# Attention and ELU MLP on one core: a later table for blocks 0 and 1, other weight portions, and the first batch's work spread otherwise over the engines

## The chip, the core and the metric

The kernel runs on one core of a Trainium2 chip. The metric is device time in microseconds (us), the median of several executions. A separate execution was recorded by the profiler; its views (busy time, waits, the chain of waits, the timeline) are what the prediction reads. Engines are named as in the profile: PE (matmul; PEld its weight loads), DVE (VectorE), ACT (ScalarE), POOL (GpSimd) and SP, which here only issues DMAs.

## What is computed

```
q, k, v: [8, 8, 576, 64] f32 (batch, heads, sequence, head dim)
q_s = softmax(q) over the 64 of head dim
k_s = softmax(k) over the sequence
kv  = k_s^T v                      # 64 x 64 per batch and head
x   = q_s kv, heads side by side   # 4608 x 512
h   = x @ w_in                     # w_in 512 x 2048
g   = h if h > 0 else exp(h) - 1
out = g @ w_out                    # w_out 2048 x 512, f32
```

## The kernel before

**Tiling.** A batch has 576 rows of q, k and v: 512 main rows as 128 partitions of four (R = 4), and 64 rest rows. Heads 0 to 3 are part A, heads 4 to 7 part B, the rest rows part R ("M" is A and B together, "C" is B and R). The MLP runs in nine blocks j: blocks 0 to 7 take the 512 main rows of a batch, block 8 the rest rows of all batches (XTR). A block has 16 steps s, one for each 128 columns of the hidden layer.

**A step.** `hidden` (L520): four matmuls into a bank of HB (three banks), exp on ACT into ES (L528), ES - 1 on POOL (L529). `elu` (L544): DVE combines bank and ES into GT (L550). `project` (L554): four matmuls into the four banks OB, three steps later (LAG = 3). A bank of HB comes free with the GT of its chunk, so `hidden` of step s waits for `elu` of step s - 3. At a block's end `store` copies the four banks on ACT and DVE and sends them.

**The next batch, beside these steps.** While block j runs, batch j + 1 is prepared. For k: `kmax` on DVE (per part A or B three instructions of 128x256, L198 to L203; for R two of 64x256, L209) into KA; `kturn` on PE (L218) into the shared bank AB; `kacross` (DVE, L226) takes the maxima over the turned partitions into NM; `kdiag` (DVE, L241) writes them on diagonals, DG; `kspread` (PE, L249) spreads them back; `ksub` (DVE, L261, L268), `kexp` (ACT, L278). `vconv` (ACT, L344, L348) casts v to VB. `kv_mm` (PE, L367) makes kv in the bank AB, `kv_fac` (DVE, L380, L384) scales and masks it into MB. For q: `qmax` (DVE, L403), `qsub` (POOL, L411), `qexp` (ACT, L417), `qsum` (DVE, L421, L423), `qmul` and `qmul_rest` (POOL, L434, L440) into QS and QSR; `qturn` (SP, L450, L454) is a DMA transpose into QW and QWR, `qwide` (ACT, L485, L489) widens that into QT and QTR; `attend` (PE L495, copy L501) makes a fourth of XT, `attend_rest` (L509, L514) the part of XTR.

**Order.** Every engine runs its instructions in the order in which the program emits them; waits are on semaphores that a small table of readers and writers puts in. The order is written out by hand: `first_batch` (L762) for batch 0, and then per step `hidden`, `project`, `step_pe`, `early`, `store`, `attend_rest`, `elu`, the weights, and one of `step_late` (blocks 0 and 1) and `step` (later blocks), `step_ahead` (block 1 on). In the first batch k is subtracted on PE (`kraw_first`, `kmin_first`) and q turned on PE (`qturn_first`, `qwide_first`).

**Queues.** SP issues the loads of q, k and v, the transposes and the stores, in order. POOL issues the weights (`load_w1`, `load_w2`; the arguments are the first and last chunk), between its own instructions. KR and QR have two buffers, VR has one.

Of the kernel before, what the change touches and what calls it, by code (L numbers as in the profile page):

```python
# [3 lines left out]
AF = mybir.ActivationFunctionType  # L4
# [5 lines left out]
F16 = mybir.dt.float16  # L10

B, H, S, D = 8, 8, 576, 64
# [3 lines left out]
R = 4  # L16
# [7 lines left out]
AB = 7  # L24
# [11 lines left out]
class Gen:  # L36
# [297 lines left out]
    def vconv(self, b, part, en="act"):  # L334
        a = self.E["act"]
        VR = self.VR[0]
        if part in "AB":
            h0 = 0 if part == "A" else 4
            vv = VR[:, 4 * h0:4 * h0 + 16, :].rearrange("p (h r) d -> p h r d", r=R)
            out = self.VB[:, :, h0:h0 + 4, 0:64].rearrange("p r h d -> p h r d")  # L340
            if en == "gp":
                self.op("gp", lambda: self.E["gp"].tensor_copy(out, vv), [f"VR0{part}"], [f"VB{part}"])  # L342
                return
            self.op("act", lambda: a.activation(out, vv, AF.Copy), [f"VR0{part}"], [f"VB{part}"])  # L344
        else:
            for i in range(2):
                sl = slice(64 * i, 64 * i + 64)
                self.op("act", lambda: a.activation(self.VBR[sl, i, :, 0:64],  # L348
                                                    VR[sl, 32:36, :], AF.Copy),
                        [f"VR0R{i}"], [f"VBR{i}"])  # L350
# [106 lines left out]
    def qturn_first(self, part, bank):  # L457

        pe = self.E["pe"]
        hh = 0 if part == "A" else 1  # L460
        ps = self.bank[bank][:, :].bitcast(F16)

        def mm():
            for j in range(2):
                for r in range(R):
                    o = (j * R + r) * 128
                    last = pe.transpose(ps[:, o:o + 128], self.QS[hh][:, r, 2 * j:2 * j + 2, :]
                                        .rearrange("p u d -> p (u d)"), self.ID16[:, :])
            return last
        self.op("pe", mm, [f"QS{part}", "ID16"], [f"bank{bank}"])  # L470

    def qwide_first(self, part, bank):
        a = self.E["act"]
        hh = 0 if part == "A" else 1
        src = self.bank[bank][:, :].bitcast(F16).rearrange("p (j t) -> p j t", j=2)
        self.op("act", lambda: a.activation(self.QT[:, 2 * hh:2 * hh + 2, :], src, AF.Copy),
                [f"bank{bank}"], [f"QT{part}"])

    def qwide(self, part):
        a = self.E["act"]  # L480
# [105 lines left out]
    def early(self, j, s):  # L586

        if j + 1 < B:
            if s == (1 if j < 2 else 0):
                self.kacross()  # L590
            if s == (2 if j < 2 else 1):
                self.kdiag()
            if s == 9:
                self.kv_fac("A", AB)
            if s == 10:
                self.kv_fac("B", AB)

    def step_pe(self, j, s):
        n = j + 1
        if j == 0 and s == 8:  # L600
            self.attend_rest(0, AB)
        if n < B:
            if s == (1 if j < 2 else 0):
                self.kturn()
            if s == (3 if j < 2 else 4):
                self.kspread()
            if s == 9:
                self.kv_mm("A", AB)
            if s == 10:
                self.kv_mm("B", AB)  # L610
            if s >= 12:
                self.attend(n, s - 12, AB)

    def weights_last(self, s):
        if s == 0:
            self.load_w1(10, 13)
        if s == 1:
            self.load_w1(13, 16)
        if s == 2:
            self.load_w2(10, 16)  # L620

    def step_late(self, j, s):

        n, m = j + 1, j + 2
        if s == 0:
            if j == 1:
                self.kmax(n, "B")
            self.kmax(n, "R")
            if j == 0:
                self.qmax(0, "R")  # L630
        if s == 1:
            if j == 1:
                self.qwide("R")
            self.qmax(n, "A")
            if j == 0:
                self.qsub(0, "R")
        if s == 2:
            if j == 0:
                self.qexp(0, "R")
            self.qmax(n, "C")  # L640
            self.qsub(n, "A")
        if s == 3:
            self.vconv(n, "A")
            if j == 0:
                self.qsum(0, "R")
            else:
                self.load("K", 3, "MR")
            self.ksub(n, "A")
            self.qsub(n, "C")
        if s == 4:  # L650
            self.qexp(n, "A")
            self.ksub(n, "B")
            if j == 0:
                self.qmul_rest(0)
            else:
                self.load("Q", 3, "MR")
        if s == 5:
            self.kexp(n, "A")
            self.vconv(n, "R")
            self.ksub(n, "R")  # L660
            if j == 0:
                self.qturn("R")
        if s == 6:
            self.qexp(n, "C")
            self.qsum(n, "A")
        if s == 7:
            self.kexp(n, "B")
            if j == 0:
                self.qwide("R")
            self.qsum(n, "C")  # L670
            self.qmul(n, "A")
        if s == 8:
            self.kexp(n, "R")
            self.vconv(n, "B")
        if s == 9:
            self.qturn("A")
            if j == 1:
                self.load("V", m, "MR")
            self.qmul(n, "B")
        if s == 10:  # L680
            self.qmul_rest(n)
        if s == 11:
            self.qwide("A")
            self.qturn("B")
            self.qturn("R")
        if s == 13:
            self.qwide("B")
        if j == 0:
            if s == 11:
                self.load("K", 2, "MR")  # L690
            if s == 12:
                self.load("Q", 2, "MR")
            if s == 13:
                self.load("V", 2, "RM")
            if s == 15:
                self.kmax(2, "A")

    def step(self, j, s):
        n, m = j + 1, j + 2
# [62 lines left out]
    def first_batch(self):  # L762

        self.kraw_first("A", (0, 1))
        self.kmax(0, "A")
        self.kmax(0, "B")
        self.kmax(0, "R")
        self.qmax(0, "A")
        self.qsub(0, "A")
        self.kturn()  # L770
        self.kraw_first("B", (2, 3))
        self.kraw_first("R", (4,))
        self.kacross()
        self.kdiag()
        self.kmin_first("A", (0, 1))
        self.kmin_first("R", (4,))
        self.kmin_first("B", (2, 3))
        self.vconv(0, "R")
        self.qexp(0, "A")
        self.qmax(0, "B")  # L780
        self.load_w1(0, 3)
        self.qsub(0, "B")
        self.kexp_first("A", (0, 1))
        self.kexp_first("R", (4,))
        self.qsum(0, "A")
        self.qmul(0, "A", "dve")
        self.vconv(0, "A", "gp")
        self.load_w2(0, 2)
        self.vconv(0, "B", "gp")
        self.load_w1(3, 6)  # L790
        self.load("V", 1, "RM")
        self.qexp(0, "B")
        self.kexp_first("B", (2, 3))
        self.qturn_first("A", 5)
        self.qwide_first("A", 5)
        self.qsum(0, "B")
        self.qmul(0, "B")
        self.kv_mm("A", 7)
        self.kv_fac("A", 7)
        self.kv_mm("B", 4)  # L800
        self.attend(0, 0, 5)
        self.attend(0, 1, 7, "dve")
        self.kv_fac("B", 4)
        self.load_w2(2, 6)
        self.load_w1(6, 10)
        self.qturn_first("B", 6)
        self.qwide_first("B", 6)
        self.attend(0, 2, 3)
        self.attend(0, 3, 4, "dve")
        for c in range(len(HB)):  # L810
            self.hidden_mm(0, c, range(2))
        self.load_w2(6, 10)

    def program(self):
        self.alloc()
# [5 lines left out]
        self.load("Q", 1, "MR")  # L821
        self.init()
        self.first_batch()
        self.kmax(1, "A")
        self.kmax(1, "B")

        steps = [(j, s) for j in range(B + 1) for s in range(NCH)]
        for i in range(len(steps) + LAG):
# [5 lines left out]
                self.project(pj, ps)  # L834
            if i < len(steps):
                self.step_pe(j, s)
                self.early(j, s)
            if i >= LAG and ps == NCH - 1:
                self.store(pj)
            if i < len(steps):  # L840
                if 0 < j < B and s == 2:
                    self.attend_rest(j, AB)
                self.elu(j, s)
                if j == 0 and s < 3:
                    self.weights_last(s)
                if j < 2:
                    self.step_late(j, s)
                else:
                    self.step(j, s)
                if j > 0:  # L850
                    self.step_ahead(j, s)
# [38 lines left out]
```

## Time and profile before

| | us |
|---|---|
| device time, median of 3 runs | 338.16 (336.59 to 339.66) |
| device time of the profiled execution | 338.62 |
| its span, first to last instruction | 336.8 |
| PE busy | 310.1 (92%) |
| DVE, ACT, POOL busy | 233.3, 188.0, 170.2 |
| first exp of block 0 (ACT L528) | 28.60 |
| first GT of block 0 (DVE L550) | 30.02 |
| first matmuls of block 1, of block 2 | 66.65, 104.56 |

The busy shares are means over the whole span. The prediction reads them by stage, since only the first two blocks are edited.

### The profile page before, as it was taken

To read this page: it belongs to the slowest core of one execution; us is meant where nothing else is said; L and a number is where in the kernel's file an instruction comes from. 1 tells how busy PE (TensorE), PEld (TensorE's weight loads), DVE (VectorE), ACT (ScalarE), POOL (GpSimd) and SP (SyncE) were. 2 spreads that over 40 slices of the span, in tenths; PEclk is the share of its full clock that TensorE was granted. 3 is DMA by queue.
4 is the path that set the end of the run, shared out by engine and by line. 5 is a ranking of instruction groups with operands and counts; after the bars stand their busy time and mean duration, and the time that the engine had idled before them with its cause. 6 is when DMAs were issued, how large, how long until landed. Compare 5 with 4: busy or idle time off the path is not lost.

```text
span 336.8 us, 4143 instructions
## 1 busy us (share of the span) xinstructions
PE 310.1 (92%) x1447; PEld 245.1 (73%) x1447; DVE 233.3 (69%) x382; ACT 188.0 (56%) x298; POOL 170.2 (51%) x204
## 2 busy tenths in 40 slices
PE   4677869979998999999999999999999999999993
PEld 1355647767776888787878887888788778888882
DVE  5937784388988797978897789778977344335342
ACT  1542484637647855686568557856785553334331
POOL 1784855227662666366537653755465333333330
PEclk9957998999999999999999999999999999999998
DMA  8999983958798367436733682371033011003003
GB/s 247 315 339 355 379 213 70 287 137 247 190 207 254 125 170 190 133 127 171 208 113 126 172 235 86 125 184 28 9 116 63 10 65 63 0 0 127 0 0 126
DMA packets 65173, 50.60 MB, mean 150 GB/s; under 512 B 31360, under 2 KB 57984, under 8 KB 65152
## 3 DMA queue, kind: packets, MB, share of 16 engines
q1 hardware_dynamic: 60080, 41.43, 44.4%
q0 software_dynamic: 4752, 8.39, 8.3%
q10 hardware_dynamic: 320, 0.52, 0.5%
q8 instruction: 11, 0.18, 0.2%
q14 instruction: 10, 0.08, 0.1%
HBM read 36.70 MB, written 9.44 MB: 137 GB/s over the span
## 4 chain that ended last, share of the span: by engine, by line
PE 77%; DMA 12%; DVE 6%; ACT 2%; POOL 1%; issue 1%; SPq 1%; DVEq 0%
PE bank L540 35%; PE bank L560 35%; DMA VR<-in_v_dram 6%; DMA QW<-QS 2%; PE bank L367 2%; PE bank L495 2%; DMA QWR<-QSR 2%; DMA KR<-in_k_dram 2%; DVE QM L403 1%; PE bank L218 1%; PE bank L509 1%; DVE GT L550 1%; DVE DG L241 1%; DVE QZ L421 1%; POOL QS L434 1%
## 5 line engine op out<-in xcount | busy, mean ns | idle before, releaser
L529 POOL TENSOR_SCALAR ES<-ES 128x512 f32<-128x512 f32 x144 | 92.5, 643 | 144.8 <-ACT ES L528 144.7
L560 PE MATMUL bank<-W2S,GT 128*128 128x512 f32 x576 | 155.6, 392 | 0.4 <-DVE OSB L571 0.4
L550 DVE SCALAR_TENSOR_TENSOR GT<-bank,ES 128x512 fp32r<-128x512 f32 x144 | 98.4, 683 | 73.0 <-PE bank L540 53.3
L540 PE MATMUL bank<-XT,W1S 128*128 128x512 f32 x512 | 144.4, 403 | 1.0 <-DVE GT L550 1.0
L528 ACT ACTIVATE ES<-bank 128x512 f32<-128x512 f32 x144 | 86.1, 598 | 104.9 <-PE bank L540 104.2
L560 PEld LDWEIGHTS bank<-W2S,GT 128*128 128x128 f32 x576 | 108.6, 189 | 24.4 <-DVE OSB L571 1.1
L540 PEld LDWEIGHTS bank<-XT,W1S 128*128 128x128 f32 x512 | 95.4, 191 | 23.0 <-ACT XT L501 3.0
L411 POOL TENSOR_TENSOR QR<-QR,QM 128x1024 f32<-128x1024 f32 (+2 forms) x17 | 34.7, 2042 | 11.0 <-DVE QM L403 10.9
L434 POOL TENSOR_TENSOR QS<-QR,QI 128x1024 f16<-128x1024 f32 x15 | 28.6, 1907 | 2.1 <-DVE QI L423 2.0
L501 ACT ACTIVATE XT<-bank 128x512 fp32r<-128x512 f32 x30 | 18.0, 599 | 15.8 <-PE bank L495 15.1
L403 DVE TENSOR_REDUCE QM<-QR 128x16 f32<-128x1024 f32 (+2 forms) x17 | 21.6, 1273 | 0.1
L421 DVE TENSOR_REDUCE QZ<-QR 128x16 f32<-128x1024 f32 (+2 forms) x17 | 21.6, 1272 | 0.0
L417 ACT ACTIVATE QR<-QR 128x1024 f32<-128x1024 f32 (+2 forms) x17 | 18.8, 1104 | 1.6 <-POOL QR L411 1.5
L344 ACT ACTIVATE VB<-VR 128x1024 bf16<-128x1024 f32 x14 | 14.8, 1059 | 5.1 <-DMA VR<-in_v_dram 5.0
L540 PE MATMUL bank<-XTR,W1S 128*128 128x512 f32 x64 | 17.1, 389 | 0.0
L261 DVE TENSOR_TENSOR KR<-KR,bank 128x1024 f32<-128x1024 f32 x14 | 16.9, 1208 | 0.0
L495 PE MATMUL bank<-QT,MB 128*128 128x512 f32 x32 | 14.0, 449 | 2.7 <-ACT QT L485 1.4
L198 DVE TENSOR_TENSOR KA<-KR 128x256 f32<-128x256 f32 x16 | 14.6, 911 | 2.5 <-DMA KR<-in_k_dram 2.5
L485 ACT ACTIVATE QT<-QW 128x1024 fp32r<-128x1024 f16 x14 | 14.7, 1051 | 1.5 <-DMA QW<-QS 1.5
L278 ACT ACTIVATE EK<-KR 128x1024 bf16<-128x1024 f32 x14 | 14.7, 1050 | 0.0
L540 PEld LDWEIGHTS bank<-XTR,W1S 128*128 128x128 f32 x64 | 12.0, 188 | 2.5
L367 PE MATMUL bank<-VB,EK 128*128 128x132 bf16 x128 | 12.5, 239 | 0.9 <-POOL VB L342 0.6
(62 smaller groups left out, 186.5 us busy)
## 6 DMA issues: line engine op xcount, KB each, us to landing
out_dram<-OSB SPq DMA_DIRECT2D x32, 256.0 KB, 2.8
KR<-in_k_dram SPq DMA_DIRECT2D x7, 1024.0 KB, 5.9
QR<-in_q_dram SPq DMA_DIRECT2D x7, 1024.0 KB, 7.8
VR<-in_v_dram SPq DMA_DIRECT2D x7, 1024.0 KB, 6.2
W1S<-in_moe_w_in_dram POOLq DMA_DIRECT2D x4, 768.0 KB, 10.8
W2S<-in_moe_w_out_dram POOLq DMA_DIRECT2D x2, 1024.0 KB, 12.7
W2S<-in_moe_w_out_dram POOLq DMA_DIRECT2D x1, 1536.0 KB, 14.7
KR<-in_k_dram SPq DMA_DIRECT2D x2, 512.0 KB, 4.5
```

The costliest lines, as they stand in the source:

```text
L367: pe.matmul(o, self.EK[:, r, h:h + 2, :].rearrange("p u d -> p (u d)"), self.VB[:, r, h:h + 2, :].rearrange("p u c -> p (u c)"), start=(r ...
L403: self.op("dve", lambda: v.tensor_reduce(self.QM[:, g], QR[:, g, :], AX.X, ALU.max), self.qkeys(b, part), self.qstat("QM", part))
L411: self.op("gp", lambda: e.tensor_tensor(QR[:, g, :], QR[:, g, :], m, ALU.subtract), keys + self.qstat("QM", part), keys)
L417: self.op("act", lambda: a.activation(QR[:, g, :], QR[:, g, :], AF.Exp), keys, keys)
L421: self.op("dve", lambda: v.tensor_reduce(self.QZ[:, g], QR[:, g, :], AX.X, ALU.add), self.qkeys(b, part), self.qstat("QZ", part))
L434: self.op(en, lambda: e.tensor_tensor(out, src, z, ALU.mult), keys[:1] + [f"QI{part}"], [f"QS{part}"])
L495: self.op("pe", lambda: pe.matmul(self.bank[bank][:, :], mb, self.QT[:, f, :], start=True, stop=True), [f"MB{f}", f"QT{part}"], [f"bank{ba ...
L528: self.op("act", lambda: a.activation(ES[:, :], ps, AF.Exp), [f"bank{bank}"], [ek])
L529: self.op("gp", lambda: g.tensor_scalar(ES[:, :], ES[:, :], -1.0, 1.0, ALU.add, ALU.mult), [ek], [ek])
L540: return pe.matmul(ps, self.W1S[:, kc, c * 128:(c + 1) * 128], x[:, kc, :], start=(kc == 0), stop=(kc == 3))
L550: self.op("dve", lambda: v.scalar_tensor_tensor(self.GT[n % NG][:, :], ps, 0.0, ES[:, :], ALU.max, ALU.min), [f"bank{bank}", ek], [f"GT{n ...
L560: return pe.matmul(self.bank[OB[t]][:, :], self.GT[n % NG][:, t * 128:(t + 1) * 128], self.W2S[:, c, :], start=(c == 0), stop=(c == NCH - 1))
```

## The change

Blocks 0 and 1 get other steps for most of the next batch's work: the k maxima stand in steps 0 (A), 1 (B) and 2 (R) instead of before the steps and in 0, or at the end of the block before; `kturn` in 4 (was 1), `kacross`, `kdiag` and `kspread` in 5 (were 1, 2 and 3), the `kv` pair in 10 and 11 (was 9 and 10). `kacross` and `kdiag` of step 5 are emitted ahead of `kspread` and of the step's `elu`. The casts of v, the q work and some loads move along.

In the first batch, `kdiag` goes to ACT (four instructions), the two casts of v from POOL to DVE, `qmul` of part A from DVE to POOL and of part B from POOL to DVE, the copy of `attend` 1 from DVE to ACT. The rest rows of q are prepared before the steps, not in steps 0 to 7; they are turned on PE in step 2 (not by a DMA) and attended in step 3 (was 8). The six early `hidden_mm` stand ahead of attends 2 and 3.

The weights are issued in ten loads instead of nine: three before the steps (were six), the others in steps 0, 1, 3, 6 and 7.

```diff
--- before.py
+++ after.py
@@ -338,8 +338,8 @@
             h0 = 0 if part == "A" else 4
             vv = VR[:, 4 * h0:4 * h0 + 16, :].rearrange("p (h r) d -> p h r d", r=R)
             out = self.VB[:, :, h0:h0 + 4, 0:64].rearrange("p r h d -> p h r d")
-            if en == "gp":
-                self.op("gp", lambda: self.E["gp"].tensor_copy(out, vv), [f"VR0{part}"], [f"VB{part}"])
+            if en == "dve":
+                self.op("dve", lambda: self.E["dve"].tensor_copy(out, vv), [f"VR0{part}"], [f"VB{part}"])
                 return
             self.op("act", lambda: a.activation(out, vv, AF.Copy), [f"VR0{part}"], [f"VB{part}"])
         else:
@@ -457,24 +457,30 @@
     def qturn_first(self, part, bank):
 
         pe = self.E["pe"]
-        hh = 0 if part == "A" else 1
         ps = self.bank[bank][:, :].bitcast(F16)
+        src = self.QSR[:, :, :].unsqueeze(1) if part == "R" else self.QS["AB".index(part)][:, :, :, :]
+        n = src.shape[1]
 
         def mm():
             for j in range(2):
-                for r in range(R):
-                    o = (j * R + r) * 128
-                    last = pe.transpose(ps[:, o:o + 128], self.QS[hh][:, r, 2 * j:2 * j + 2, :]
+                for r in range(n):
+                    o = (j * n + r) * 128
+                    last = pe.transpose(ps[:, o:o + 128], src[:, r, 2 * j:2 * j + 2, :]
                                         .rearrange("p u d -> p (u d)"), self.ID16[:, :])
             return last
         self.op("pe", mm, [f"QS{part}", "ID16"], [f"bank{bank}"])
 
     def qwide_first(self, part, bank):
         a = self.E["act"]
-        hh = 0 if part == "A" else 1
-        src = self.bank[bank][:, :].bitcast(F16).rearrange("p (j t) -> p j t", j=2)
-        self.op("act", lambda: a.activation(self.QT[:, 2 * hh:2 * hh + 2, :], src, AF.Copy),
-                [f"bank{bank}"], [f"QT{part}"])
+        ps = self.bank[bank][:, :].bitcast(F16)
+        if part == "R":
+            out = self.QTR[:, :, :].rearrange("p (hh j) t -> p j hh t", hh=2)
+            src, key = ps[:, 0:256].rearrange("p (j hh t) -> p j hh t", j=2, hh=2), "QTR"
+        else:
+            hh = 0 if part == "A" else 1
+            out, key = self.QT[:, 2 * hh:2 * hh + 2, :], f"QT{part}"
+            src = ps[:, :].rearrange("p (j t) -> p j t", j=2)
+        self.op("act", lambda: a.activation(out, src, AF.Copy), [f"bank{bank}"], [key])
 
     def qwide(self, part):
         a = self.E["act"]
@@ -586,96 +592,93 @@
     def early(self, j, s):
 
         if j + 1 < B:
-            if s == (1 if j < 2 else 0):
+            late = j < 2
+            if s == (5 if late else 0):
                 self.kacross()
-            if s == (2 if j < 2 else 1):
+            if s == (5 if late else 1):
                 self.kdiag()
-            if s == 9:
+            if s == (10 if late else 9):
                 self.kv_fac("A", AB)
-            if s == 10:
+            if s == (11 if late else 10):
                 self.kv_fac("B", AB)
 
     def step_pe(self, j, s):
         n = j + 1
-        if j == 0 and s == 8:
+        if j == 0 and s == 2:
+            self.qturn_first("R", 6)
+            self.qwide_first("R", 6)
+        if j == 0 and s == 3:
             self.attend_rest(0, AB)
         if n < B:
-            if s == (1 if j < 2 else 0):
+            late = j < 2
+            if s == (4 if late else 0):
                 self.kturn()
-            if s == (3 if j < 2 else 4):
+            if s == (5 if late else 4):
+                if late:
+                    self.early(j, s)
                 self.kspread()
-            if s == 9:
+            if s == (10 if late else 9):
                 self.kv_mm("A", AB)
-            if s == 10:
+            if s == (11 if late else 10):
                 self.kv_mm("B", AB)
             if s >= 12:
                 self.attend(n, s - 12, AB)
 
-    def weights_last(self, s):
+    def weights(self, s):
         if s == 0:
-            self.load_w1(10, 13)
+            self.load_w2(3, 6)
         if s == 1:
-            self.load_w1(13, 16)
-        if s == 2:
-            self.load_w2(10, 16)
+            self.load_w1(6, 9)
+        if s == 3:
+            self.load_w2(6, 9)
+            self.load_w1(9, 12)
+        if s == 6:
+            self.load_w1(12, 16)
+            self.load_w2(9, 12)
+        if s == 7:
+            self.load_w2(12, 16)
 
     def step_late(self, j, s):
 
         n, m = j + 1, j + 2
         if s == 0:
-            if j == 1:
-                self.kmax(n, "B")
-            self.kmax(n, "R")
-            if j == 0:
-                self.qmax(0, "R")
+            self.kmax(n, "A")
         if s == 1:
             if j == 1:
                 self.qwide("R")
+            self.kmax(n, "B")
+        if s == 2:
+            self.kmax(n, "R")
+        if s == 3:
+            self.vconv(n, "R")
             self.qmax(n, "A")
-            if j == 0:
-                self.qsub(0, "R")
-        if s == 2:
-            if j == 0:
-                self.qexp(0, "R")
+            if j == 1:
+                self.load("K", 3, "MR")
+        if s == 4:
+            self.vconv(n, "A")
             self.qmax(n, "C")
             self.qsub(n, "A")
-        if s == 3:
-            self.vconv(n, "A")
-            if j == 0:
-                self.qsum(0, "R")
-            else:
-                self.load("K", 3, "MR")
+        if s == 5:
+            self.vconv(n, "B")
             self.ksub(n, "A")
             self.qsub(n, "C")
-        if s == 4:
+        if s == 6:
             self.qexp(n, "A")
             self.ksub(n, "B")
-            if j == 0:
-                self.qmul_rest(0)
-            else:
+        if s == 7:
+            self.qexp(n, "C")
+            self.ksub(n, "R")
+            self.qsum(n, "A")
+            if j == 1:
                 self.load("Q", 3, "MR")
-        if s == 5:
+        if s == 8:
             self.kexp(n, "A")
-            self.vconv(n, "R")
-            self.ksub(n, "R")
-            if j == 0:
-                self.qturn("R")
-        if s == 6:
-            self.qexp(n, "C")
-            self.qsum(n, "A")
-        if s == 7:
-            self.kexp(n, "B")
-            if j == 0:
-                self.qwide("R")
             self.qsum(n, "C")
             self.qmul(n, "A")
-        if s == 8:
+        if s == 9:
             self.kexp(n, "R")
-            self.vconv(n, "B")
-        if s == 9:
+            self.kexp(n, "B")
             self.qturn("A")
-            if j == 1:
-                self.load("V", m, "MR")
             self.qmul(n, "B")
         if s == 10:
             self.qmul_rest(n)
@@ -683,6 +686,8 @@
             self.qwide("A")
             self.qturn("B")
             self.qturn("R")
+            if j == 1:
+                self.load("V", m, "MR")
         if s == 13:
             self.qwide("B")
         if j == 0:
@@ -692,8 +697,6 @@
                 self.load("Q", 2, "MR")
             if s == 13:
                 self.load("V", 2, "RM")
-            if s == 15:
-                self.kmax(2, "A")
 
     def step(self, j, s):
         n, m = j + 1, j + 2
@@ -771,45 +774,47 @@
         self.kraw_first("B", (2, 3))
         self.kraw_first("R", (4,))
         self.kacross()
-        self.kdiag()
+        self.kdiag("act")
         self.kmin_first("A", (0, 1))
         self.kmin_first("R", (4,))
         self.kmin_first("B", (2, 3))
-        self.vconv(0, "R")
+        self.qmax(0, "B")
+        self.qsub(0, "B")
         self.qexp(0, "A")
-        self.qmax(0, "B")
         self.load_w1(0, 3)
-        self.qsub(0, "B")
         self.kexp_first("A", (0, 1))
         self.kexp_first("R", (4,))
+        self.vconv(0, "R")
         self.qsum(0, "A")
-        self.qmul(0, "A", "dve")
-        self.vconv(0, "A", "gp")
-        self.load_w2(0, 2)
-        self.vconv(0, "B", "gp")
-        self.load_w1(3, 6)
+        self.qmul(0, "A")
+        self.vconv(0, "A", "dve")
+        self.vconv(0, "B", "dve")
         self.load("V", 1, "RM")
         self.qexp(0, "B")
         self.kexp_first("B", (2, 3))
+        self.kv_mm("A", 7)
+        self.kv_fac("A", 7)
         self.qturn_first("A", 5)
         self.qwide_first("A", 5)
         self.qsum(0, "B")
-        self.qmul(0, "B")
-        self.kv_mm("A", 7)
-        self.kv_fac("A", 7)
+        self.qmul(0, "B", "dve")
+        self.load_w2(0, 3)
+        self.load_w1(3, 6)
         self.kv_mm("B", 4)
+        self.kv_fac("B", 4)
         self.attend(0, 0, 5)
-        self.attend(0, 1, 7, "dve")
-        self.kv_fac("B", 4)
-        self.load_w2(2, 6)
-        self.load_w1(6, 10)
+        self.attend(0, 1, 7)
         self.qturn_first("B", 6)
         self.qwide_first("B", 6)
+        self.qmax(0, "R")
+        self.qsub(0, "R")
+        for c in range(len(HB)):
+            self.hidden_mm(0, c, range(2))
         self.attend(0, 2, 3)
         self.attend(0, 3, 4, "dve")
-        for c in range(len(HB)):
-            self.hidden_mm(0, c, range(2))
-        self.load_w2(6, 10)
+        self.qexp(0, "R")
+        self.qsum(0, "R")
+        self.qmul_rest(0)
 
     def program(self):
         self.alloc()
@@ -821,8 +826,6 @@
         self.load("Q", 1, "MR")
         self.init()
         self.first_batch()
-        self.kmax(1, "A")
-        self.kmax(1, "B")
 
         steps = [(j, s) for j in range(B + 1) for s in range(NCH)]
         for i in range(len(steps) + LAG):
@@ -834,15 +837,16 @@
                 self.project(pj, ps)
             if i < len(steps):
                 self.step_pe(j, s)
-                self.early(j, s)
+                if not (j < 2 and s == 5):
+                    self.early(j, s)
             if i >= LAG and ps == NCH - 1:
                 self.store(pj)
             if i < len(steps):
                 if 0 < j < B and s == 2:
                     self.attend_rest(j, AB)
                 self.elu(j, s)
-                if j == 0 and s < 3:
-                    self.weights_last(s)
+                if j == 0:
+                    self.weights(s)
                 if j < 2:
                     self.step_late(j, s)
                 else:
```

## The prediction

> **What bounds the kernel now.** I read the table of busy time by stage first. Columns: the stretch, its length, busy time of PE, PE's weight loads, DVE, ACT and POOL, the granted clock, the DMA share and the GB/s.
>
> ```profile
> 0.00:28.40 28.40, 18.38 (x69) 11.64 (x70) 18.69 (x41) 9.81 (x14) 14.45 (x20) 0.79 1.08 305
> 28.40:62.00 33.60, 26.45 (x123) 20.15 (x122) 21.74 (x36) 17.55 (x28) 20.56 (x23) 0.93 0.87 244
> 62.00:92.00 30.00, 27.59 (x128) 21.14 (x126) 22.83 (x38) 18.76 (x31) 15.56 (x17) 1.00 0.79 215
> ...
> 124.97:157.95 32.98, 32.98 (x162) 26.57 (x162) 27.65 (x44) 22.36 (x35) 19.09 (x22) 1.00 0.54 156
> ```
>
> From 125 us PE is busy all of a block's 32.98 us. So whatever the change saves or costs in blocks 0 and 1, which it alone edits, arrives at the end unchanged. In the timeline the matmuls of block 1 step 0 (after the fourth "attend") begin at 66.65, those of block 2 at 104.56: block 1 takes 37.9, 4.9 over the later block. Second view: PE's own waits from 28 to 125 us.
>
> ```profile
> PE bank L218 <- DVE KA L209: 4.1, 2, 2.4
> PE bank L509 <- ACT QTR L489: 2.9, 1, 2.9
> PE bank L495 <- ACT QT L485: 1.4, 1, 1.4
> PE bank L540 <- DVE GT L550: 1.0, 1, 1.0
> ```
>
> The k turn waits for the k maxima once per block (2.4 at 29.4, 1.7 at 70.8); the remainder's attention waits 2.9 at 46.5; late q transposes cost 1.4 at 100.7. The 1.0 at 41.5 goes back to ACT, which stood 4.95 us before the V cast. The chain of waits says for what:
>
> ```profile
> 19.95 19.50 DMA VR<-in_v_dram
> ...
> 42.33 6.46 DMA QWR<-QSR
> ```
>
> Batch 1's V needs 19.5 us to land, since 3 MB of weights are issued from POOL at 21.6 to 23.1 and share the DMA engines. The second line is the remainder's DMA transpose, behind the 2.9 us wait. A table of 2 us stretches shows that wait's second price:
>
> ```profile
> 50.00:52.00 2.00, 2.00 (x7) 1.53 (x7) 0.69 (x1) 1.99 (x4) 0.42 (x1) 0.62 0.59 113
> 52.00:54.00 2.00, 2.00 (x14) 1.48 (x13) 0.00 (x0) 0.14 (x1) 1.78 (x2) 0.53 0.09 18
> ```
>
> After it the clock is at about half for some 3.7 us: 1.85 us lost. Last, the timeline, for two DVE instructions beside one POOL instruction each:
>
> ```profile
> 9.75 1.90 POOL L411 TENSOR_TENSOR QR<-QR,QM 128x1024 f32<-128x1024 f32 x1 [7.80 <-DVE QM L403]
> 10.35 1.85 DVE L241 TENSOR_TENSOR DG<-ID,NM 128x512 fp32r<-128x512 f32 x1
> ...
> 97.15 1.91 POOL L411 TENSOR_TENSOR QR<-QR,QM 128x1024 f32<-128x1024 f32 x1 [0.19 <-DVE QM L403]
> ...
> 97.67 1.67 DVE L198 TENSOR_TENSOR KA<-KR 128x256 f32<-128x256 f32 x1
> ```
>
> L241 alone takes 0.68, L198 0.42; both here end just after POOL's instruction.
>
> **First batch.** The 1.85 of kdiag goes from DVE to four ACT copies of 128x128. Nearest ACT rows: 0.41 (128x256), 0.60 (x512), 1.05 (x1024), so about 0.3 each, 1.2 in all (at most 4 x 0.41 = 1.64). DVE is free at 10.3, so qmax B ends at 11.6 and POOL's qsub B follows qsub A: 11.65 to 13.55. The first W1 load moves behind it, from 11.59 to 13.55; its kind landed in 8.5 to 9 us, so about 22.3. Its first user comes at about 22.4: no cost, up to 0.5 otherwise. POOL's two V casts (2.02 and 1.05) go to DVE: between 0.7 (half of L261's 1.21 and a start) and 1.21; I take 0.9. qmul A goes to POOL (1.9), qmul B to DVE (1.62 beside POOL in the trace, 1.2 alone by L261). The chain to QS B on DVE: qsum A ends 14.3, V cast 0.9, POOL's qmul A holds it 1.9, V cast 0.9, kv_fac A 0.8, qsum B 1.45, qmul B 1.4: 21.65, as now (21.66). From there the six early matmuls fill the 1.0 us widening and the first exp comes about 6.2 later instead of 6.9. The remainder's sub, exp, sum and multiply now stand before the steps: qmul_rest ends at about 28.55 and POOL's first ES after it, so the first GT starts at 29.2 instead of 30.02. Gain 0.8 (0 to 1.7).
>
> **Block 0 up to the spread.** The new order puts this on DVE before kdiag of step 5: five GTs (0.69), six k maxima of 0.42, two of 0.42 for the rest, qmax 1.21 and 1.48, kacross 0.69, kdiag 0.68: 10.9. Consecutive ones overlap (three maxima take 1.13, not 1.26), so 10.1. The maxima have both inputs in SBUF and run beside POOL's ES (0.62): I add 0.3 for each third, 0.9, bounds 0 and 4.6 (the longest L198, L200, L203, L209 rows: 1.67, 0.83, 0.71, 0.75). kdiag ends at 29.2 + 11.0 = 40.2. PE has until then three hidden and three project groups, turn and remainder, done by about 36.4; it waits 3.8 us, and chunk 6 starts at 40.65 against 39.58 now: 1.1 lost. What is queued behind kspread on PE is everything, and ksub on DVE waits for it too.
>
> **Block 0 after it.** Now: 66.65 - 39.58 = 27.1 us. Work in it: ten steps of 1.82, two kv of 0.6, four attends of 0.23: 20.3. Gone are the wait for V (its rivals on the DMA engines are now 2.25 MB, then loads issued from step 0; with some 9 MB at 350 GB/s it lands by 29, its cast comes after 32), the 2.9 us, since the remainder is turned by PE in step 2 (two transposes by L467's 0.13, one copy of 0.4) and attended in step 3. Not gone: the half clock after a 3.8 us wait, 1.85. New: QS A comes some 10 us after kspread (ksub, GT, qsum and two weight issues on POOL before it), the transpose lands 3.0 to 7.8 later (its range), the copy takes 1.05; attend needs it 14.3 after. I take 0.5 (0 to 4.6), as it is nearest to the 3.2 median. So 20.3 + 2.35 = 22.6, and block 1 starts at 63.25 instead of 66.65: 3.4 gained.
>
> **Weights.** Ten issues instead of nine, 0.75 to 0.98 each on POOL. They delay ES in steps 0, 1, 3, 6 and 7 by up to 1.6; DVE is behind by more than that, so nothing, or 0.8 if DVE catches up. W1 6 to 9 is issued at about 31 and needed at 40.6; no load of this size took above 13.1 when all ran together.
>
> **Block 1.** PE reaches the spread after six steps of 1.82, turn 0.42, remainder 0.35, the XT wait 0.28 and the store's wait 0.4: 12.3. DVE starts its first GT 2.65 after the block (matmul, exp, ES), does the same 10.1 and two store copies (1.28): 14.0, plus 0.6 for POOL. PE waits 2.3. The late transposes of 100.7 had V's load issued before them; now V comes behind them in SP's queue; 0.4 left. Excess 2.7 instead of 4.9: 2.2 gained. Moving K and Q loads on SP costs nothing: K3 is first used at step 12. With batch 2's K sent at about 55 and the K loads' median of 5.9, its maxima (66 on) don't wait.
>
> **Sum.** 3.4 + 2.2 = 5.6 from the profiled execution's 338.62 (span 336.8, 1.8 around it): 333.0. That execution is 0.46 above the median, so 332.6.
>
> [...]
>
> **The rivals.** *Only kdiag is caught.* In step 5, counted from qmax A's end, DVE reaches kdiag after GT 0.6, qmax C 1.4 and kacross 0.66: 2.66. POOL reaches qsub C after qsub A 1.9 and ES 0.62, with hops 2.65. A tie: if POOL is first, kdiag waits some 2.0 of its 2.34. For it: 10.35 above; against: at 34.88 kdiag came first and POOL waited. Once: 334.6; in both blocks, with the half clock in block 1 as well, 338.5. *The lock at every maximum* (slower): with the longest rows each block pays 3.9 for six, 0.7 for two and 1.17 for kdiag: 5.8 instead of the 1.5 I took for both. 332.6 - 1.5 + 11.6, and 1.85 of half clock in block 1: 344.5. It turns to slower by 1% from about 5 us per block. For it: L198's median in the trace is 0.82; against: in blocks 0 and 1 POOL has only ES of 0.62 in steps 0 to 2. *V or transposes stay late:* V landing at 39 again, or the transpose at 7.8, costs 4 to 5: 337.
>
> **Chances.** Forecast, with its better bounds (no half clock, no lock: down to 328.5): 0.56. Kdiag caught once 0.08, half of that under 334.8. Caught twice or late transfers 0.2. Lock everywhere 0.16. What a measurement can tell is about 1%, 3.4 us: faster 0.6, within 0.24, slower 0.16. The range 328.5 to 341.5 leaves out most of the last case and little below.
>
> **What would show it.** Right: V no longer in the chain, no wait of PE at L509 behind QTR, a wait at L249 for kdiag of 2 to 4 us in each of blocks 0 and 1, GT of chunk 0 near 29.2, block 1 starting near 63, block 2 near 99. Wrong: kdiag ending after 42, maxima above 0.8, weights in PE's waits, ACT waiting for QW by several us.

## The result, and the profile after

The changed kernel takes 340.83 us (median of 17 runs, 339.21 to 342.16) against 338.16 of the kernel before (17 runs): a ratio of 1.0069, 95% interval 1.0045 to 1.0093. By the ratio it is slower by about 2.3 us; the forecast was 332.6. The profiled execution took 340.83, its span is 339.0.

The table of busy time by stage of the changed kernel (columns as before), cut where blocks 1 and 2 begin:

```profile
0.00:28.40 28.40, 18.64 (x71) 11.24 (x72) 17.17 (x38) 12.06 (x21) 10.63 (x17) 0.82 1.07 306
28.40:66.78 38.38, 30.84 (x142) 23.71 (x141) 27.63 (x41) 20.14 (x32) 23.76 (x29) 0.91 0.87 234
66.78:106.76 39.98, 35.92 (x162) 27.95 (x161) 32.88 (x50) 22.30 (x35) 20.89 (x23) 0.91 0.71 186
106.76:139.90 33.14, 33.14 (x163) 26.72 (x162) 28.17 (x46) 22.33 (x35) 18.96 (x22) 1.00 0.75 212
```

Block 1 starts at 66.78 (before 66.65) and takes 39.98 (before 37.91); from block 2 on PE is busy without a break. So all of the loss is in block 1, and what was to be gained in block 0 is not there. PE's own waits from 20 to 130 us (total, times, longest):

```profile
PE bank L249 <- DVE DG L241: 8.8, 2, 4.8
PE bank L546 <- DMA W1S<-in_moe_w_in_dram: 1.4, 1, 1.4
PE bank L546 <- DVE GT L556: 1.1, 1, 1.1
PE bank L218 <- DVE KA L209: 1.1, 1, 1.1
...
```

The waits for the remainder (2.9 in block 0) and for the late transposes of block 1 (1.4) are gone, and so is V from the chain of waits. In their place stands one wait per block at the spread, L249, for the diagonals, L241: 4.76 and 4.01. The timeline shows what the diagonals wait for, in block 0 and again in block 1:

```profile
39.41 0.61 POOL L535 TENSOR_SCALAR ES<-ES 128x512 f32<-128x512 f32 x1
39.99 2.32 POOL L411 TENSOR_TENSOR QR<-QR,QM 128x1280 f32<-128x1280 f32 x1
40.06 2.79 DVE L241 TENSOR_TENSOR DG<-ID,NM 128x512 fp32r<-128x512 f32 x1
...
42.91 0.79 PE L249 MATMUL bank<-DG,ONES 128*128 128x512 f32 x1 [4.76 <-DVE DG L241]
...
80.66 2.33 POOL L411 TENSOR_TENSOR QR<-QR,QM 128x1280 f32<-128x1280 f32 x1
80.75 2.79 DVE L241 TENSOR_TENSOR DG<-ID,NM 128x512 fp32r<-128x512 f32 x1
...
83.59 0.79 PE L249 MATMUL bank<-DG,ONES 128*128 128x512 f32 x1 [4.01 <-DVE DG L241]
```

In block 0 of the kernel before, the diagonals came first, and POOL's subtraction (there part A) 0.3 after them:

```profile
34.88 0.68 DVE L241 TENSOR_TENSOR DG<-ID,NM 128x512 fp32r<-128x512 f32 x1
35.18 2.14 POOL L411 TENSOR_TENSOR QR<-QR,QM 128x1024 f32<-128x1024 f32 x1
```

In the changed kernel POOL's second q subtraction (part C) starts 0.07 and 0.09 us ahead of the diagonals, which then take 2.79 instead of 0.68. They end 0.54 after POOL's instruction: most of their own 0.68 is still to be done when POOL's instruction ends. "The lock" is the name for this hold-up, 2.79 for 0.68, here and in the prediction. The table of 2 us stretches shows what the wait does to the clock (the third number from the right):

```profile
40.00:42.00 2.00, 0.00 (x0) 0.00 (x0) 1.97 (x2) 0.00 (x0) 2.00 (x2) 0.65 0.12 25
42.00:44.00 2.00, 1.09 (x3) 0.90 (x4) 1.71 (x3) 0.00 (x0) 0.30 (x1) 0.50 0.00 0
44.00:46.00 2.00, 2.00 (x6) 1.58 (x5) 0.97 (x1) 0.55 (x2) 0.00 (x0) 0.50 0.00 0
46.00:48.00 2.00, 2.00 (x7) 1.54 (x6) 1.15 (x2) 0.99 (x2) 1.87 (x3) 0.64 0.00 0
...
80.00:82.00 2.00, 0.00 (x0) 0.00 (x0) 1.97 (x3) 0.25 (x1) 2.00 (x3) 0.89 1.08 311
82.00:84.00 2.00, 0.41 (x1) 0.41 (x2) 2.00 (x2) 0.00 (x0) 0.99 (x1) 0.50 1.12 285
84.00:86.00 2.00, 2.00 (x6) 1.52 (x6) 1.36 (x2) 0.00 (x0) 0.00 (x0) 0.50 1.01 287
86.00:88.00 2.00, 2.00 (x6) 1.54 (x5) 0.47 (x1) 1.54 (x2) 0.62 (x1) 0.50 0.19 43
88.00:90.00 2.00, 2.00 (x9) 1.63 (x8) 1.35 (x2) 0.91 (x2) 0.23 (x1) 0.90 0.00 0
```

The granted clock falls to 0.50 of full speed, so twice the missing clock of such rows is the time at half clock: 2 x 2 x (0.35 + 0.5 + 0.5 + 0.36) = 6.84 in each of the two blocks, of which PE works 4.5 to 4.8 and so loses some 2.3.

### The profile page after: what moved, and what is told of

Its sections match the earlier page's. It is cut to its first block, busy times and chain, and to the rows that moved or that the text cites. A ratio compares the mean times of both kernels' runs of the same rounds, so it can differ in the third digit from the quotient of the medians.

```text
span 339.0 us, 4151 instructions
## 1 busy us (share of the span) xinstructions
PE 312.0 (92%) x1449; PEld 246.2 (73%) x1449; DVE 238.6 (70%) x382; ACT 189.5 (56%) x303; POOL 167.3 (49%) x203
## 4 chain that ended last, share of the span: by engine, by line
PE 80%; DVE 8%; DMA 6%; POOL 2%; issue 1%; SPq 1%; ACT 0%; DVEq 0%
PE bank L546 38%; PE bank L566 36%; DMA W1S<-in_moe_w_in_dram 3%; PE bank L501 2%; DVE QM L403 2%; PE bank L367 2%; DVE DG L241 2%; DVE GT L556 2%; DMA QR<-in_q_dram 1%; DMA QW<-QS 1%; POOL QR L411 1%; PE bank L249 1%; PE bank L515 1%; PE bank L218 1%; POOL QS L434 1%
## 5 line engine op out<-in xcount | busy, mean ns | idle before, releaser
L546 PE MATMUL bank<-XT,W1S 128*128 128x512 f32 x512 | 146.4, 406 | 2.8 <-DMA W1S<-in_moe_w_in_dram 1.4
L546 PEld LDWEIGHTS bank<-XT,W1S 128*128 128x128 f32 x512 | 96.4, 193 | 25.9 <-ACT XT L507 4.0
L411 POOL TENSOR_TENSOR QR<-QR,QM 128x1024 f32<-128x1024 f32 (+2 forms) x17 | 34.0, 2005 | 15.5 <-DVE QM L403 15.5
L198 DVE TENSOR_TENSOR KA<-KR 128x256 f32<-128x256 f32 x16 | 15.6, 978 | 2.3 <-DMA KR<-in_k_dram 2.3
L367 PE MATMUL bank<-VB,EK 128*128 128x132 bf16 x128 | 11.6, 228 | 1.8 <-DVE VB L342 1.8
```

The costliest lines, as they stand in the source:

```text
L411: self.op("gp", lambda: e.tensor_tensor(QR[:, g, :], QR[:, g, :], m, ALU.subtract), keys + self.qstat("QM", part), keys)
L546: return pe.matmul(ps, self.W1S[:, kc, c * 128:(c + 1) * 128], x[:, kc, :], start=(kc == 0), stop=(kc == 3))
```

## The experiments

The theory after the result (A): the diagonals lose a race of under 0.1 us to POOL's subtraction in each block; that costs 2.1 us, and through the longer idle time the clock. The rivals: the late place of the spread costs by itself, and another wait takes over without the lock (B); or the new first batch and weights cost (C). Every ratio is to the kernel before, on the same chip.

**The diagonals first.** POOL's second subtraction also reads DG, so that it comes behind the diagonals; nothing else is changed.

```diff
             self.ksub(n, "A")
-            self.qsub(n, "C")
+            self.qsub(n, "C", ["DG"])
```

> The changed kernel, with one wait added: in blocks 0 and 1 POOL's second q subtraction (part C) waits for the diagonals, so that DVE's diagonal instruction comes first. Theory A (the lock at the diagonals is the cost): L241 falls from 2.79 to about 0.7 in both blocks, PE's waits at L249 from 4.8 and 4.0 to about 2.6 and 1.9, and the half clock after block 1's wait (2.3 us) goes with it: 340.8 - 4.2 - 2.3 = 334.3, or 332.1 if block 0's half clock goes too, 336.6 if both stay. Rival B (the late place itself costs, another wait takes over): not under 339.

Measured: 335.25, ratio 0.9901 (0.9863 to 0.9938). The timeline of this run in block 0:

```profile
40.60 0.69 DVE L241 TENSOR_TENSOR DG<-ID,NM 128x512 fp32r<-128x512 f32 x1
...
41.35 0.50 PE L249 MATMUL bank<-DG,ONES 128*128 128x512 f32 x1 [2.67 <-DVE DG L241]
41.38 2.33 POOL L411 TENSOR_TENSOR QR<-QR,QM 128x1280 f32<-128x1280 f32 x1 [0.82 <-DVE DG L241]
```

The diagonals take 0.69 in both blocks, PE's waits fall to 2.67 and 1.93 as A said, and the time falls by 5.6 us: the 4.2 of the lock and part of the half clock. One added wait on POOL is worth more than the whole loss of the change. B falls: no wait took over. (The ten runs spread from 332.7 to 335.8, and the profiled one, 335.49, is among the longer.) The half clock is not gone but shorter:

```profile
42.00:44.00 2.00, 2.00 (x8) 1.60 (x7) 1.10 (x1) 1.21 (x2) 2.00 (x2) 0.68 0.02 5
44.00:46.00 2.00, 2.00 (x6) 1.54 (x6) 1.60 (x2) 0.33 (x1) 1.78 (x3) 0.50 0.08 6
46.00:48.00 2.00, 2.00 (x10) 1.68 (x9) 0.69 (x2) 1.76 (x2) 1.19 (x2) 0.97 0.95 304
```

That is 2 x 2 x (0.32 + 0.5 + 0.03) = 3.4 instead of 6.84; block 1 shows 3.4 too, after a wait of only 1.93.

**The diagonals on ACT.** The other way out of the lock: POOL still starts its subtraction first, but the diagonals are made by an engine beside it.

```diff
-                self.kdiag()
+                self.kdiag("act" if late else "dve")
```

> The changed kernel with the diagonals of blocks 0 and 1 written by ACT (four copies, 1.28 in the first batch's trace) and nothing else moved. [...] Rival B: not under 339.

Measured: 335.69, ratio 0.9928 (0.9900 to 0.9955). A gives 337.8 if the diagonals come 1.5 earlier in each block (340.8 - 3.0), and 335.5 if the half clock of block 1 goes as well: the time is at the better end. That POOL would not hold up ACT was the author's estimate; the trace of block 0 bears it out.

```profile
40.13 2.32 POOL L411 TENSOR_TENSOR QR<-QR,QM 128x1280 f32<-128x1280 f32 x1
40.20 1.28 ACT L235 ACTIVATE DG<-ID,NM 128x128 fp32r<-128x128 f32 x4 [2.19 <-DVE NM L226]
...
41.62 0.77 PE L249 MATMUL bank<-DG,ONES 128*128 128x512 f32 x1 [3.33 <-ACT DG L235]
```

POOL's instruction runs as long as before beside it, and ACT's four copies take the same 1.28 as in the first batch: it is DVE and POOL that exclude each other here (DVE's diagonals took 2.79 for 0.68 behind POOL's subtraction, and the subtraction 2.14 for 1.90 where the diagonals had begun 0.3 before it, at 35.18 in the kernel before), and the subtraction's mere presence does not hold up the diagonals. One half-clock stretch is left (3.4 us in block 0), none in block 1, in its profile.

**Half the change each.** First the new first batch and weights with the old step table. The edit: the old `early`, `step_pe` and `step_late`, without the rest rows' q work, and in the first batch

```diff
         self.qsub(0, "R")
+        self.kmax(1, "A")
+        self.kmax(1, "B")
         for c in range(len(HB)):
```

> The first batch and the weight portions of the change, with the step table of the kernel before (the rest rows of q prepared early as in the change, attended in step 8; the k maxima of batch 1, parts A and B, on DVE while it waits for attend 2). Theory A (only the new table costs, the rest of the change gains): the wait for V (1.0), the wait for the remainder (2.9) and its half clock (1.85) go, and the start comes 0.6 earlier: 338.2 - 6.3 = 331.9, range 330 to 334. Rival C (first batch or weights cost): not under 338.

Measured: 335.09, ratio 0.9918 (0.9884 to 0.9952). The sign is A's, and C falls for the first batch and the weights taken together; the size is 3 us short of the 331.9. PE's waits show where:

```profile
PE bank L218 <- DVE KA L209: 4.5, 2, 2.8
PE bank L546 <- DMA W1S<-in_moe_w_in_dram: 1.9, 1, 1.9
```

The waits for V and the remainder are gone, but the first weights now come 1.9 late, and the k turn of block 0 still waits 2.8. During and after that wait the clock was half for 6.84 us (30.0 to 36.9), against 3.4 in block 0 of the kernel before.

Then the new table alone, with the old first batch and weights (the mirrored edit):

> The kernel before with only the new step table (its own first batch, weights and late rest rows). Theory A: the diagonals are caught behind POOL in both blocks or at least wait as late as in the changed kernel, and V is late as before: slower than the changed kernel's 340.8, 341 to 345. Rival C: the table costs nothing, 337 to 339.

Measured: 339.55, ratio 1.0077 (1.0038 to 1.0117). Neither range held; by the ratio it can't be told apart from the changed kernel (1.0069). The race is lost in both blocks, by 0.09 and 0.08. In block 0:

```profile
42.29 2.33 POOL L411 TENSOR_TENSOR QR<-QR,QM 128x1280 f32<-128x1280 f32 x1
42.38 2.78 DVE L241 TENSOR_TENSOR DG<-ID,NM 128x512 fp32r<-128x512 f32 x1
...
45.22 0.79 PE L249 MATMUL bank<-DG,ONES 128*128 128x512 f32 x1 [5.27 <-DVE DG L241]
```

Its ten runs fall into 338.5 to 340.4 and 342.3 to 342.8, and the profile is of an upper one; what divides them was not tried. Together the two halves give: the table costs 0.8%, the rest gains 0.8%, both cost 0.7%. So the rest's gain hardly shows on top of the table. One reason is in the waits: with the table alone PE waits only 0.2 for the remainder, where the kernel before waited 2.9, so both halves take away the same wait. The rest is open. In the profiled execution the other half of the change does bring the spread of block 0 forward, from 45.22 to 42.91; no execution of the lower group was profiled.

**The first weights early.** On the first experiment's kernel, the first W1 load is again issued before POOL's second subtraction of batch 0.

```diff
         self.qmax(0, "B")
+        self.load_w1(0, 3)
         self.qsub(0, "B")
         self.qexp(0, "A")
-        self.load_w1(0, 3)
```

> Run e1 with the first W1 load issued before POOL's second q subtraction of batch 0, as in the kernel before. If the load's place cost what the profile shows, PE's wait for W1S (1.9 in e1, 1.4 in the changed kernel) falls under 0.5 and the time by about 1.4 to 333.9; part B of q comes some 0.4 later. Rival: the attends' chain is as late as the load, and nothing changes (335.3).

Measured: 331.67, ratio 0.9825 (0.9790 to 0.9861): a gain of 3.6 over the first experiment where 1.4 was expected (the two intervals lie just apart). Two lines of PE's timeline, first of the kernel with the diagonals first, then of this one:

```profile
23.06 2.93 PE L546 MATMUL bank<-XT,W1S 128*128 128x512 f32 x6 [1.86 <-DMA W1S<-in_moe_w_in_dram]
```

```profile
21.74 1.64 PE L546 MATMUL bank<-XT,W1S 128*128 128x512 f32 x6
```

The six early matmuls start 1.3 earlier and run at full clock, in 1.64 instead of 2.93. But the wait did not go as expected: 1.75 of it moved to the second W1 load, at 28 us. Most of the difference seems to lie in the clock. The profile of the first experiment shows half clock from 22.2 to 29.1 and for 3.4 us in each of the two blocks; this one shows it from 17.2 to 20.6 and for 3.4 us in block 0 alone. These are 6.8 us less at half clock, worth up to 3.4 of the 3.8 between the two profiled executions. Whether the load's place brings that about in every run, or by luck in this one, was not tried; the last section has what stood ahead of such stretches in the nine profiles.

**The maxima early.** On top, k maxima of parts A and B of batch 1 go into the time in which DVE waits for attend 2, R into step 0, those of batch 2 a step earlier.

```diff
         self.qsub(0, "R")
+        self.kmax(1, "A")
+        self.kmax(1, "B")
         for c in range(len(HB)):
...
         if s == 0:
-            self.kmax(n, "A")
-        if s == 1:
             if j == 1:
-                self.qwide("R")
-            self.kmax(n, "B")
-        if s == 2:
+                self.kmax(n, "B")
+            else:
+                self.kmax(n, "R")
+        if s == 1 and j == 1:
+            self.qwide("R")
             self.kmax(n, "R")
...
+            if s == 15:
+                self.kmax(2, "A")
```

> Run e5 with the k maxima drawn forward: batch 1's parts A and B into the time in which DVE waits for attend 2 (21.5 to 26.7), R into step 0; batch 2's part A into step 15 of block 0, B and R into steps 0 and 1. Theory (the rest of the wait at the spread is DVE's list): L249's waits fall from 2.7 and 1.9 to about 0.4 and 0.8, both half clocks go: 333.9 - 2.3 - 1.8 - 1.1 - 1.65 = 327, to 330 if the half clocks stay. Rival (another wait takes over at the same step, such as POOL's ES or the exp): 333 or more.

Measured: 330.38, ratio 0.9797 (0.9756 to 0.9838), not clearly apart from the run before it. The waits at the spread fell only to 1.83 and 1.70, and one half-clock stretch stayed. The time in which DVE waits had been read in the changed kernel; in the kernel that was edited it is much shorter. DVE's copy of the last part of XT, first in the changed kernel, then in the run with the first weights early:

```profile
26.68 0.69 DVE L504 CAST XT<-bank 128x512 fp32r<-128x512 f32 x1 [5.23 <-PE bank L501]
```

```profile
23.89 0.69 DVE L504 CAST XT<-bank 128x512 fp32r<-128x512 f32 x1 [1.58 <-PE bank L501]
```

The maxima now stand before this copy, and PE waits 0.84 for it, so that the first GT starts at 27.94 instead of 26.60 in the run before: of the 2.3 us that the expectation took from DVE's list ahead of the spread, 1.3 are given back at its beginning. No wait took over at the spread itself; a new one came ahead of it.

**A mixed table.** Block 0 by the old table, with all three maxima ahead of the steps; block 1 by the run just told.

```diff
+        self.kmax(1, "A")
+        self.kmax(1, "B")
+        self.kmax(1, "R")
         for c in range(len(HB)):
...
-            if s == (4 if late else 0):
+            if s == (1, 4, 0)[min(j, 2)]:
                 self.kturn()
-            if s == (5 if late else 4):
+            if s == (3, 5, 4)[min(j, 2)]:
...
                 self.kspread()
```

> Block 0 by the table of the kernel before (run e3's, with all three maxima of batch 1 ahead of the steps), block 1 by run e6's; first W1 load early. e3 waited 2.8 at the k turn of block 0 and ran 6.6 us at half clock there, 1.9 for W1; all three should go: 335.1 - 2.8 - 3.3 - 1.4 = 327.6, and about 0.5 in block 1: 327 to 330. Rival (DVE or POOL take over in steps 1 to 3): 332 or more.

Measured: 330.00, ratio 0.9777 (0.9743 to 0.9811), the fastest, though not apart from the run before it. Block 0 shows no half clock any more:

```profile
28.40:62.00 33.60, 30.21 (x144) 22.77 (x143) 22.35 (x36) 20.62 (x33) 23.63 (x28) 1.00 1.03 289
```

PE works 30.2 of these 33.6 us at full clock; before it was 26.5 at 0.93. Block 1 still waits 1.7 at the spread.

## Why the prediction was wrong

**The step that failed** is the sum's silent choice at the tie. The prediction worked out that DVE reaches the diagonals 2.66 after qmax A and POOL its second subtraction 2.65 after it, called it a tie, and then summed as if DVE won in both blocks. It gave 0.08 to losing once and 0.2 to losing twice or late transfers. The runs show 2.62 (40.06 against the end of qmax A at 37.44) and 2.55 (39.99): POOL was ahead by 0.07, 0.09, 0.09 and 0.08 in all four blocks looked at with this table (two kernels). A tie that repeats in each block from the same durations is one throw, not two, and its loss belonged in the forecast. The price was right: 2.1 per block against 2.0.

"Kdiag caught in both blocks" was worked out as 338.5, and 340.8 came. Of the difference, 0.9 is the half clock, taken at 1.85 in each block and 2.3 in the profile; 0.6 is the later start of the diagonals in block 0, 0.2 the lock; and the forecast took off 0.46 for a profiled execution above the median, which that of the changed kernel is not. The 1.85 itself was read a little high: by the rows of the kernel before the clock was at half for 3.4 us, not 3.7. The range, up to 341.5, holds the result only by the room that it left for the rivals.

**Block 0 up to the spread.** Right but for the lock: the first GT at 29.38 (29.2 foretold), the diagonals start at 40.06 (39.5). The start held for another reason than given: QS B was done at 20.4, earlier than the 21.65, but the first weights landed at 22.82 and PE waited 1.37 for them, where I had allowed 0 to 0.5. The load took 9.57 where I had 8.5 to 9, and its users came 0.9 sooner. The fifth experiment gained 3.6 by moving this load alone, up to 3.4 of it by the clock.

**Block 0 after it.** V no longer stands in the chain of waits and the remainder costs PE no wait any more, as said. The transposes landed in 4.2 and cost PE 0.6 (0.5 said). From chunk 6, at 43.51, to block 1 it took 23.3 against 22.6; the half clock (2.3 instead of 1.85) is most of the difference.

**Block 1.** The diagonals start 13.97 after the block's start, 13.92 by the sum. Then 2.1 of lock and 2.3 of half clock that the sum didn't have: 39.98 instead of 35.7, the 4.3 that are missing. The sum had charged the half clock after block 0's wait but none after the 2.3 that it foresaw in block 1, without giving a reason; with the lock gone 1.93 us of waiting still brought one in the run with the diagonals first.

**The lock at the maxima.** At the diagonals the traces show it: 2.79 beside POOL's subtraction, 0.69 once the order is turned. DVE's GT, which reads a bank, took its usual 0.69 beside the same subtraction (at 40.26 in the run with the diagonals on ACT). The rival that let the lock catch every maximum as well did not come: the first instruction of each group of three took 1.00 and 0.81 in block 0, 0.42 and 0.41 in block 1, against 0.42 alone. The 1.0 us that this adds in block 0 is about the 0.9 that the sum had.

**Without the lock** the forecast would still have been too low: 335.25 against 332.6. By the rows of that run the late first load (1.9) and the half clock of block 1 (1.7) more than cover the rest; with the load early as well, and no half clock in block 1, 331.67 came.

## What to carry to other kernels

Where the trace shows two engines excluding each other (2.79 for 0.68 here) and a hand-written order lets both arrive within 0.1 us, give the one that others wait for a fixed place: one extra wait on the other engine was worth 5.6 us here. Sum a wait of PE with what it may do to the clock behind it, as a range (none to 6.84 us at half clock here). Read a gap that you want to fill in the kernel that you edit: 5.2 us in one trace were 1.6 in the next, and of the 2.3 us of work moved into it 1.3 came back.

## What the runs showed of the hardware

The half clock came in steps. By twice the missing clock of the rows it lasted 3.4 us in block 0 of the kernel before, 3.4 in each of both blocks with the diagonals first, 3.4 with them on ACT, and 6.84 in both blocks of the changed kernel and in block 0 of the run with the old table: one unit or two. In the first batch it lasted three units in the changed kernel (10.2) and four in the kernel before (13.7). The starts show the same unit. In the changed kernel the stretches begin at 16.71, 40.60 and 81.56: 23.89 and 40.96 apart, 7 and 12 times 3.413 (40.96 / 12). With the diagonals first they begin at 22.24, 42.72 and 80.28: 20.48 and 37.56 apart, 6 and 11 times it within 0.02.

So the time after the first stretch is cut here into units of 3.413 us, and PE's idle time read in each (the unit's length less PE's busy time, the first number after the comma). Block 1 of the changed kernel:

```profile
78.15:81.56 3.41, 1.44 (x7) 0.83 (x5) 3.38 (x4) 1.54 (x2) 3.35 (x3) 1.00 1.02 287
81.56:84.98 3.42, 1.39 (x3) 1.16 (x4) 3.13 (x3) 0.00 (x0) 1.43 (x1) 0.50 1.11 299
84.98:88.39 3.41, 3.41 (x9) 2.63 (x8) 1.52 (x3) 1.54 (x2) 0.62 (x1) 0.50 0.39 95
```

Block 1 of the run with the first weights early:

```profile
71.80:75.22 3.42, 2.04 (x10) 1.36 (x8) 3.38 (x5) 2.12 (x3) 2.68 (x3) 1.00 1.00 251
75.22:78.63 3.41, 2.86 (x13) 2.37 (x14) 2.30 (x3) 1.41 (x2) 2.83 (x2) 1.00 1.12 303
78.63:82.04 3.41, 3.41 (x17) 2.83 (x16) 3.16 (x5) 3.08 (x5) 1.21 (x3) 1.00 0.58 160
```

Both blocks by this reading (us), for those waits at the spread that differ most:

| kernel, block | PE's wait | idle in the units that it touches | half clock |
|---|---|---|---|
| changed kernel, 0 | 4.76 | 2.44 and 2.30 | two units |
| changed kernel, 1 | 4.01 | 1.97 and 2.02 | two units |
| new table alone, 0 | 5.27 | 1.89 and 3.37 | one unit |
| new table alone, 1 | 4.03 | 1.12 and 2.90 | one unit |
| diagonals on ACT, 1 | 2.60 | 0.84 and 1.76 | none |
| diagonals first, 1 | 1.93 | 1.91 | one unit |
| first weights early, 1 | 1.93 | 1.37 and 0.55 | none |

In all nine profiles, for units that begin between 26 and 120 us: a unit at full clock with 1.9 us or more of idle time (1.91 to 3.37) was followed by one at half clock (one with 1.89 was not), a unit at full clock with 1.76 or less never was, and between these both happened (1.83 was, in block 0 of the run with the maxima early; 1.85 was not, in block 0 of the kernel before). Units at half clock were followed by another after 1.32, 2.02 and 2.30 us of idle time. In these profiles idle time far under one unit was thus enough. Of two waits of 1.93 us, the one that fell into one unit (1.91, diagonals first) had a unit at half clock behind it, and the one divided between two (1.37 and 0.55, first weights early) had none. Such a unit costs up to 1.7 us: in the two tables above, one in which PE never stops has 9 matmuls at half clock and 17 at full. That the division decides is a reading of these profiles; no run varied it alone. Where the units lie differs between the nine profiles and was not under control here. The second unit of half clock in each block of the changed kernel is in this sense chance; the 2.1 us of the lock in each block are not.
